# A delta-rule attention with a feed-forward block: from step 7 on most scores are computed a step later, and the queries' transposes in pairs behind later small runs

## Chip, cores, metric

One core of a Trainium2 chip runs the kernel. The metric is the device time of one execution in microseconds; runs of a kernel are given by their median. The engines are named as the profile names them: PE is TensorE (PEld its weight loads), DVE is VectorE, ACT is ScalarE, POOL is GpSimd, and SP is the queue that issues most DMAs.

## What is computed

```python
batch, n_heads, seq, head_dim = (4, 8, 768, 48)
k_n = k / (norm(k, axis=-1) + 1e-06)
state = zeros((B, H, D, D))
for t in range(S):
    y[:, :, t] = einsum('bhd,bhde->bhe', q[:, :, t], state)
    v_old = einsum('bhde,bhd->bhe', state, k_n[:, :, t])
    state = state + beta[t] * einsum('bhd,bhe->bhde', k_n[:, :, t], v[:, :, t] - v_old)
x = y.transpose(0, 2, 1, 3).reshape(B * S, H * D)      # 3072 x 384
h = x @ w_in                                           # 384 x 2048
out = (h * clip(h + 3, 0, 6) / 6) @ w_out              # 2048 x 384
```

All data are float32.

## The kernel before

**Steps.** The sequence of 768 tokens is cut into 24 chunks of 32 tokens, and one step `t` of the recurrence treats one chunk of all 4 batches and 8 heads: 4 x 32 tokens stand on the 128 partitions. Within a chunk the recurrence becomes a triangular system. What depends on the state is in `chain(t)`: the products with the state (`ks`, L795), the right hand side `R` (L890, L898), the product with the inverse (`pz`, L816, copied by ACT at L916), the update of the state (`su`, L927, subtracted by DVE at L945), the outputs (`py`, L816, added at L852), and their transposes (`yt`, L862, copied at L866). `ks`, `pz`, `py`, `su` and the scores are small matmuls, 64 rows of each in the profile; the document calls such a stretch a small run.

**Preparation.** What does not depend on the state is done six steps ahead (`LA = 6`) by `prep(t)`: POOL normalizes the keys (L499); TensorE transposes the keys and then the queries of the chunk (`pt`, L513), four transposes each, and ACT copies each result to `KQ` (L521); TensorE forms the scores of keys with keys and with queries (`sc`, L536); DVE multiplies these by a mask with beta into `L` and `LB` (L547); POOL makes that mask (`mb`, L475) and the keys times beta (`bkb`, L487). `L` goes into an inverse that is computed for a group of four chunks (`inverse`), begun in the second step of the group before; `LB` is used in the output `py`. Groups are chunk 0, then 1-4, 5-8, 9-12, 13-16, 17-20, 21-23.

**Feed-forward.** Two steps make a block of 256 tokens, `mlp_units()`. From block 3 on the first product is `up_by_eleven` (L1055): `begin(j)` takes a PSUM buffer `ph`, runs four products of 128 columns, which the profile shows as eight instructions, and hands the buffer to ACT (L1069); `end(j)` adds five more, ten instructions; DVE and ACT then read it (L1082, L1086, L1089). From block 2 on the second product is `down_by_seven` (L1215): each `product` takes one buffer `po` and comes in two halves of eight instructions, with sums on DVE (L1201) and copies on ACT (L1222).

**Order.** Everything is emitted in a fixed order, and each engine works in that order. Up to step 4 it is written out as `ORDER`. From step 5 a step has 15 units, `u` = 0 to 14. In each unit the piece of `plan` for it comes first, then some loads, some DVE work of the inverse (`fill`), and then one unit of the feed-forward. From step 7 on, in odd steps the units 0 to 11 are halves of `down_by_seven`; in even steps (from 8 on) they are `begin` and `end` in turn, `begin(2)` in unit 0, `begin(4)` in unit 4, `begin(6)` in unit 8. The plan of before, with `ch` the next piece of `chain(t)` and `now` the next piece of `prep(t + 6)`: unit 0 `ks`, then the keys' transposes and the mask; unit 2 the queries' transposes, then the load of four pieces of queries on SP; unit 4 `pz` and, directly behind it, the scores; unit 5 the multiplications and `bkb`; unit 8 `su` and `py`; unit 9 the output sum and the state; unit 10 `yt`; unit 13 the next chunk's keys are normalized. In the steps 8 and 12 (`APART`) the scores stand alone in unit 6 and the multiplications in unit 7.

**Buffers.** PSUM is used through two rings. `pm` has four buffers of one bank, for `pt`, `pz`, `py`, `yt`, `ph`, `po`; `pc` has two buffers of two banks, for `ks`, `su` and `sc`. `ring(tag, n, key)` chooses the buffer whose last user was marked read earliest in the order of emission (`read`), and the new user's first matmul then waits until the last user's readers are done. `read` notes the first mark of a key only:

```python
i = min(range(n), key=lambda i: reads.get(held[i], len(reads)))
needs(("read", held[i]))
held[i] = key
...
past.add(("read", key))
reads.setdefault(key, len(reads))
```

In `up_by_eleven` the piece that marks `ph` of `j` as read (`first`) is emitted right after `begin(j + 2)`; `py` is marked read in unit 9, `pz` with its copy in unit 4.

Of the kernel before, what the change touches and what calls it, by code (L numbers as in the profile page):

```python
# [9 lines left out]
FP32 = mybir.dt.float32  # L10
# [4 lines left out]
ACTF = mybir.ActivationFunctionType  # L15
# [29 lines left out]
def kernel(  # L45
# [55 lines left out]
    def group(t):  # L101
        return (0, t) if t < G0 else ((t - G0) // GS + 1, (t - G0) % GS)

    def size(g):
        return G0 if g == 0 else min(GS, N - first(g))

    def first(g):
        return 0 if g == 0 else G0 + (g - 1) * GS
# [35 lines left out]
    def ring(tag, n, key):  # L144

        held = rings.setdefault(tag, [])
        i = len(held)
        if i < n:
            held.append(key)
        else:  # L150
# [3 lines that stand above are left out]
        slot[tag] = f"{tag}{i}"  # L154

    def read(*keys):
        for key in keys:
            past.add(("read", key))
            reads.setdefault(key, len(reads))
# [323 lines left out]
    def scaled(t):  # L483
# [7 lines left out]
        past.add(("bkb", t))  # L491
        yield

    def prep(t, whole=True):

        g, i = group(t)
        kb, qb = kbufs[t % NKB], qbufs[t % NQB]
        needs(*([("bkb", t - NKB)] if t >= NKB else []), *(pad(t) if t < NKB and t else []))
        nc.gpsimd.tensor_tensor(  # L499
            out=kb[:, :, 0:D], in0=kfs[g][:, i],  # L500
            in1=invs.pop(t).unsqueeze(2).to_broadcast([P, H, D]), op=ALU.mult,
        )
        past.add(("kb", t))
        yield

        for j, src in enumerate((kb, qb)):
            if j == 1:
                needs(("q", t))
                past.add(("qT", t))
            ring("pm", NPM, ("pt", t, j))  # L510
            pt = psM.tile([128, NP, P], FP32, name="pt", tag=slot["pm"])
            for p in range(NP):
                nc.tensor.transpose(  # L513
                    pt[:, p, :], src[:, 2 * p : 2 * p + 2].rearrange("p e w -> p (e w)"), ident[:]
                )
            yield 1
            if j == 0:
                ring("KQ", NKQ, ("KQ", t))
                KQ = work.tile([128, NP * B // 2, 4, C], FP32, name="KQ", bufs=NKQ)
            read(("pt", t, j))  # L520
            nc.scalar.activation(  # L521
                out=KQ[:, :, 0:4:3, :] if j == 0 else KQ[:, :, 1:3, :],
                in_=pt[:].rearrange("q p (x y c) -> q (p x) y c", y=2, c=C), func=ACTF.Copy,
            )
            if whole and j == 0:
                drain(mask(t))
            yield
        ring("pc", NPC, ("sc", t))
        sc = psC.tile([P, 2, 512], FP32, name="sc", tag=slot["pc"])
        scv = sc[:, :, 0 : NP * 2 * C].rearrange("p e (a j w) -> p e a j w", a=NP, j=2)  # L530
        for p in range(NP):
            for b in range(B):
                for e in range(2):
                    r = slice(DP * e, DP * e + DP)
                    kq = KQ[r, p * B // 2 + b // 2]
                    nc.tensor.matmul(  # L536
                        scv[rows(b), e, p],
                        lhsT=kq[:, 3 if b % 2 else 0, :],
                        rhs=kq[:, 3:1:-1, :] if b % 2 else kq[:, 0:2, :],
                        start=True, stop=True,  # L540
                    )
        yield
        needs(*([("BZ", t - NLB)] if t >= NLB else []))
        LB = work.tile([P, H, C], FP32, name="LB", bufs=NLB)
        mb = mbs.pop(t)
        for j, out in enumerate((lowers(t), LB)):
            nc.vector.tensor_tensor(  # L547
                out=out.rearrange("p (e a) w -> p e a w", e=2), in0=scv[:, :, :, j, :],
                in1=mb[:, :, :, j, :], op=ALU.mult,
            )  # L550
        past.add(("L", t))
        KQs[t], LBs[t] = KQ, LB
        read(("sc", t), *([("KQ", 0)] if t == 0 else []))
        if whole:
            drain(scaled(t))
        yield
# [204 lines left out]
        yield  # L761


    xTs, outs, zs = {}, {}, {}

    def banks(name, t, i):
        ring("pc", NPC, (name, t, i))
        return psC.tile([128, 2, 512], FP32, name=name, tag=slot["pc"])

    def he(h):  # L770
        return (h % 2) * NP + h // 2
# [558 lines left out]
    def take(gen, n=1):  # L1330
        for _ in range(n):
            while next(gen, None) == 1:
                pass

    def drain(gen):
        for _ in gen:
            pass
# [103 lines left out]
    with tc.manual_schedule():  # L1441
        for word in ORDER.split():
            word, _, n = word.partition("*")
            for _ in range(int(n or 1)):
                do(word)
        for name in relus:
            settle(0, name)
        while evicts:
            evicts.pop(0)()

        units = gens["u"]
        fill = inverse_of(2)
        loads = iter(())
        left = due = 0
        USED = {"up": 0.42, "eleven": 1.0, "down": 0.7}
        APART = (8, 12)
        CHAIN = {0: 0.45, 1: 0.75, 2: 0.75, 3: 0.4, 4: 0.4, 6: 0.5, 9: 0.8, 10: 0.6, 14: 0.2}
        for t in range(LS, N):
            g, i = group(t)
            ch = chain_of(t)  # L1460
            behind = t == LS
            now, more, third, later = (prep_of(t + LA - n) for n in (2, 1, 0, -1))
            if not behind:
                now = third
            take(gens["v"], 4)
            if i == 0:
                left += 1
            if i == 2:
                loads = keys_of(g + 3)
            plan = {  # L1470
                0: lambda: take(ch),
                1: lambda: (take(ch), take(now)),
                2: lambda: (take(ch), take(now), take(gens["q"], 4)),
                3: lambda: take(ch),
                4: lambda: (take(ch), take(now, t not in APART)),
                5: lambda: take(now, t not in APART),
                6: lambda: take(now),
                7: lambda: take(now, t in APART),
                8: lambda: take(ch),
                9: lambda: take(ch),  # L1480
                10: lambda: take(ch),
                11: lambda: token_sums(t // CB),
                13: lambda: take(later),
            }
            if not behind:
                plan.update({
                    0: lambda: (take(ch), take(now)),
                    1: lambda: take(ch),
                })
            if behind:  # L1490
                plan[13] = None
                for u, gen in zip((3, 5, 5, 6, 7, 9, 10, 11, 12, 13), (more,) * 5 + (third,) * 5):
                    plan[u] = lambda old=plan.get(u), gen=gen: (old and old(), take(gen))
            ready = (1, 6)
            for u in range(NU):
                if plan.get(u):
                    plan[u]()
                take(loads, 2)
                if (i, u) == (0, 2):
                    drain(fill)  # L1500
                    left = 0
                    fill = norms_of(g + 2)
                if (i, u) == ready:
                    drain(fill)
                    fill = inverse_of(g + 1)
                    take(fill)
                    left, due = 2 * (C - 2) + 2, 0.0
                take(rest)
                take(gens["a"])
                take(units)  # L1510
                settle(1)
                while evicts:
                    evicts.pop(0)()
                if i == 1 == ready[0] and 5 < u < 7:
                    continue
                if i == 0 or not left:
                    take(fill, 2 if i or u < 2 else u > 4)
                    continue
                room = max(1.65 - USED[mode["of"]] - CHAIN.get(u, 0), 0.15) / mode["mean"]
                due += room * left / max((GS - i) * NU - u, 1)  # L1520
                due = min(due, 2.6)
                take(fill, int(due))
                left, due = max(left - int(due), 0), due - int(due)
            if behind:
                take(later)
            drain(ch)
        for _ in units:
            settle(2)
# [30 lines left out]
```

## Time and profile before

| | |
|---|---|
| median of 3 runs | 662.84 us (662.6 to 662.97) |
| the profiled execution's own time | 661.27 us |
| its span, first to last instruction | 659.6 us |
| mean granted TensorE clock | 0.984 |
| step 8 (ks to ks) | 233.33 to 258.28 us |
| step 9 | 258.28 to 283.31 us |
| step 10 | 283.31 to 308.07 us |
| last step without preparation, 20 | 529.42 to 552.56 us |

The span is what the profiler saw between the first and the last instruction. In rows by time the columns are the start, the length, the engine, the line, the operation, the output and inputs with their shapes, the count of merged instructions, and in brackets the idle time before it with what ended it. In the windows the columns are the stretch, its length, each engine's busy time with the count of instructions, the granted TensorE clock, and the DMA share. Matmuls overlap, and their ends are modelled, so the start of the next one tells more than the length of the last.

### The profile page before, as it was taken

The numbers are of one execution on the slowest core, as the hardware profiler recorded it, in microseconds if no ns is written. First come the engines' busy times: TensorE is split into PE (matmuls) and PEld (weight loads), VectorE is DVE, ScalarE is ACT, GpSimd is POOL, SyncE is SP. The second block draws the span as 40 slices with busy tenths as digits, with TensorE's granted clock in tenths as the row PEclk, the third lists the DMA queues.
The fourth block names the chain that finished last, engine by engine and source line by source line (L and its number), as shares of the span: only waits on it lengthen the run. The fifth ranks groups of instructions, "written<-read, shape, count | busy, mean of one in ns | idle before, by whom it ended". The sixth has DMA issues, their size and how long they took to land.

```text
span 659.6 us, 26613 instructions
## 1 busy us (share of the span) xinstructions
PE 631.0 (96%) x11640; PEld 567.6 (86%) x11640; DVE 501.5 (76%) x1164; ACT 263.8 (40%) x547; POOL 226.2 (34%) x352
## 2 busy tenths in 40 slices
PE   2768999999999999999999999999999999999997
PEld 2558987776689989999999999999999999999997
DVE  5989877798658988758988858989658998456354
ACT  4786578322232154154154244244243144153240
POOL 6531023003652354553254354164051242231330
PEclk9868999999999999999999999999999999999999
DMA  7889346302050030041030030030020020000101
GB/s 175 206 200 234 79 99 162 53 24 41 17 89 14 2 75 3 3 90 22 3 74 3 2 74 3 2 63 2 3 49 3 5 47 3 23 18 2 26 1 24
DMA packets 88692, 33.28 MB, mean 50 GB/s; under 512 B 80224, under 2 KB 83424, under 8 KB 88576
## 3 DMA queue, kind: packets, MB, share of 16 engines
q1 hardware_dynamic: 88224, 31.29, 21.8%
q8 instruction: 91, 1.49, 1.0%
q10 hardware_dynamic: 352, 0.30, 0.2%
q14 instruction: 25, 0.20, 0.1%
HBM read 26.84 MB, written 4.72 MB: 48 GB/s over the span
## 4 chain that ended last, share of the span: by engine, by line
PE 91%; DVE 3%; DMA 2%; SPq 1%; issue 1%; ACT 1%; DVEq 0%
PE po L1215 28%; PE ph L1055 27%; PE ph L983 9%; PE po L1151 6%; PE ks L795 4%; PE pt L513 3%; PE su L927 3%; PE pz L816 3%; PE py L816 3%; PE sc L536 2%; PE yt L862 1%; DMA w_out<-in_moe_w_in_dram 1%; SPq L168 1%; PE pi L673 1%; DMA spare<-in_moe_w_in_dram 1%
## 5 line engine op out<-in xcount | busy, mean ns | idle before, releaser
L1055 PE MATMUL ph<-xT,w_in 128*128 128x128 f32 (+1 forms) x720 | 156.3, 320 | 0.0
L1019 POOL TENSOR_TENSOR g<-g 128x256 f32<-128x256 f32 (+1 forms) x144 | 88.0, 612 | 104.0 <-ACT g L1069 98.4
L1055 PEld LDWEIGHTS ph<-xT,w_in 128*128 128x128 f32 x720 | 116.9, 191 | 6.4
L1215 PE MATMUL po<-w_out,g 128*128 128x192 f32 x640 | 110.6, 326 | 0.0
L1215 PEld LDWEIGHTS po<-w_out,g 128*128 128x128 f32 x640 | 104.6, 190 | 0.5
L1215 PE MATMUL po<-spare,g 128*128 128x192 f32 x480 | 85.1, 331 | 0.0
L1069 ACT ACTIVATE g<-ph 128x512 f32<-128x512 f32 x72 | 43.0, 597 | 92.6 <-PE ph L1055 92.6
L1215 PEld LDWEIGHTS po<-spare,g 128*128 128x128 f32 x480 | 77.4, 190 | 1.5
L983 PE MATMUL ph<-xT,w_in 128*128 128x128 f32 (+1 forms) x384 | 72.1, 338 | 0.9 <-ACT xT L866 0.6
L1225 POOL TENSOR_TENSOR o<-o,u 128x192 f32<-128x192 f32 x18 | 13.3, 741 | 163.2 <-ACT o L1222 75.6
L983 PEld LDWEIGHTS ph<-xT,w_in 128*128 128x128 f32 x384 | 59.7, 194 | 8.4 <-ACT xT L866 0.8
L1082 DVE TENSOR_TENSOR g<-ph,g 128x256 f32<-128x256 f32 x72 | 30.2, 420 | 45.7 <-PE ph L1055 41.2
L748 DVE TENSOR_TENSOR pr<-A 128x30 f32<-128x30 f32 (+9 forms) x150 | 58.4, 389 | 3.3
L1201 DVE TENSOR_TENSOR g<-g 128x512 f32<-128x512 f32 x80 | 56.2, 724 | 3.8 <-PE po L1215 3.7
L753 DVE TENSOR_TENSOR A<-A,pr 128x30 f32<-128x30 f32 (+9 forms) x150 | 56.3, 375 | 3.3
L1102 DVE SCALAR_TENSOR_TENSOR g<-o,g 128x512 f32<-128x512 f32 x72 | 52.5, 729 | 7.4 <-ACT o L1099 7.4
L1055 PE MATMUL ph<-beta_tok,sums_in 128*128 128x128 f32 x288 | 55.7, 275 | 0.0
L1099 ACT ACTIVATE o<-g 128x512 f32<-128x512 f32 x72 | 45.4, 630 | 11.8 <-DVE g L1102 8.5
L1222 ACT ACTIVATE o<-po 128x192 f32<-128x192 f32 x40 | 13.2, 330 | 90.8 <-PE po L1215 90.8
L345 ACT ACTIVATE spare<-spare 128x768 uint16<-128x768 uint16 (+1 forms) x56 | 47.3, 850 | 3.1 <-DVE X L547 1.8
L499 POOL TENSOR_TENSOR kb<-kf,inv 128x384 f32<-128x384 f32 x24 | 21.7, 906 | 73.2 <-issue 42.6
L1151 PE MATMUL po<-w_out,g 128*128 128x384 f32 x128 | 45.4, 490 | 0.0
(137 smaller groups left out, 1010.2 us busy)
## 6 DMA issues: line engine op xcount, KB each, us to landing
kf<-in_k_dram SPq DMA_DIRECT2D x96, 48.0 KB, 2.8
qb<-in_q_dram SPq DMA_DIRECT2D x96, 48.0 KB, 2.6
vf<-in_v_dram SPq DMA_DIRECT2D x96, 48.0 KB, 2.4
out_dram<-o SPq DMA_DIRECT2D x90, 48.0 KB, 1.6
spare<-in_moe_w_in_dram SPq DMA_DIRECT2D x4, 768.0 KB, 5.4
w_out<-in_moe_w_in_dram SPq DMA_DIRECT2D x4, 768.0 KB, 6.1
w_out<-in_moe_w_out_dram SPq DMA_DIRECT2D x4, 768.0 KB, 7.4
spare<-in_moe_w_out_dram SPq DMA_DIRECT2D x4, 768.0 KB, 5.5
```

Source lines behind the costliest of these rows:

```text
L345: nc.scalar.activation(out=z, in_=z if n else d.bitcast(I16)[:, :, :, 3], func=func, bias=value, scale=scale,)
L748: nc.vector.tensor_tensor(out=pv, in0=A[:, j + 1 :, j].unsqueeze(2).to_broadcast([n, w, j]), in1=A[:, j, 0:j].unsqueeze(1).to_broadcast([n ...
L753: nc.vector.tensor_tensor(out=A[:, j + 1 :, 0:j], in0=A[:, j + 1 :, 0:j], in1=pv, op=ALU.subtract)
L983: nc.tensor.matmul(ph[:, cols], lhsT=w_in[:, s, f * 128 : (f + 1) * 128], rhs=xT[:, s, cols], start=(s == 0), stop=(s == NKT - 1),)
L1019: nc.gpsimd.tensor_tensor(out=out, in0=a, in1=b, op=op)
L1055: nc.tensor.matmul(ph[:, n], lhsT=w, rhs=x, start=start, stop=stop, skip_group_check=True)
L1069: nc.scalar.activation(out=gt, in_=ph[:], func=ACTF.Copy)
L1099: nc.scalar.activation(out=r, in_=g, func=ACTF.Relu, bias=0.5, scale=1.0 / 6.0)
L1102: nc.vector.scalar_tensor_tensor(out=g, in0=r, scalar=1.0, in1=g, op0=ALU.min, op1=ALU.mult)
L1151: nc.tensor.matmul(pos[c][:], lhsT=gs[blk, f // 2][:, f % 2, c * P : (c + 1) * P], rhs=w_out[:, f, :], start=(f == 0), stop=(f == NFC - 1),)
L1201: nc.vector.tensor_tensor(out=A(f, *out, 4), in0=A(f, *a, 4), in1=A(f, *b, 4), op=op)
L1215: nc.tensor.matmul(ps[n][:], lhsT=A(f - f % 2, *a)[:, f % 2], rhs=b[:, f], start=(f == 0), stop=(f == HF - 1),)
```

## The change

`late(t)` picks the chunks after 11 that are not the last of their group: 13, 14, 15, 17, 18, 19, 21, 22. For these:

- The queries' transposes come in two pairs, each with a `pm` buffer of its own and an ACT copy of 256 columns in place of one of 512. The first pair stands in unit 4 behind `pz`, the second in unit 8 behind `py`; the mask is made behind the second.
- The scores come in unit 0 of the next step, behind `ks` and ahead of that step's keys' transposes. The multiplications and `bkb` come in unit 5 of the next step (in unit 7 of the steps 8 and 12).
- The scores no longer use `pc`. The two buffers of `pc` are now allocated once (`halves_of_banks`); `ks` and `su` use columns 0 to 255 of each bank, late scores columns 256 to 511 by a ring of their own, `ps`. Scores that are not late still use `pc`, in columns 0 to 255.
- The load of queries moves from unit 2 to unit 9 in these steps.
- In the steps 10, 14 and 17, which prepare the last chunk of a group, the late scores of the chunk before it stand in unit 0, their multiplications and the next mask in unit 3, and the own scores behind `pz` as before.

```diff
+    def late(t):
+        g, i = group(t)
+        return LS + LA < t < first(g) + size(g) - 1
+
...
-                past.add(("qT", t))
+                if not late(t):
+                    past.add(("qT", t))
+            if j == 1 and late(t):
+                n = NP // 2
+                for p0 in range(0, NP, n):
+                    ring("pm", NPM, ("pt", t, p0))
+                    pt = psM.tile([128, n, P], FP32, name="pt", tag=slot["pm"])
+                    for p in range(n):
+                        p2 = 2 * (p0 + p)
+                        nc.tensor.transpose(
+                            pt[:, p, :], src[:, p2 : p2 + 2].rearrange("p e w -> p (e w)"), ident[:]
+                        )
+                    yield 1
+                    read(("pt", t, p0))
+                    x = B // 2
+                    nc.scalar.activation(
+                        out=KQ[:, x * p0 : x * p0 + x * n, 1:3, :],
+                        in_=pt[:].rearrange("q p (x y c) -> q (p x) y c", y=2, c=C), func=ACTF.Copy,
+                    )
+                    if p0:
+                        past.add(("qT", t))
+                        drain(mask(t))
+                    yield
+                break
             ring("pm", NPM, ("pt", t, j))
...
-            if whole and j == 0:
+            if whole and j == 0 and not late(t) and not late(t - 1):
                 drain(mask(t))
             yield
-        ring("pc", NPC, ("sc", t))
-        sc = psC.tile([P, 2, 512], FP32, name="sc", tag=slot["pc"])
+        tag, c = ("ps", 256) if late(t) else ("pc", 0)
+        ring(tag, NPC, ("sc", t))
+        sc = halves_of_banks[int(slot[tag][2:])][:, :, c : c + 256]
...
+    halves_of_banks = [psC.tile([128, 2, 512], FP32, name=f"pc{i}") for i in range(NPC)]
...
-        return psC.tile([128, 2, 512], FP32, name=name, tag=slot["pc"])
+        return halves_of_banks[int(slot["pc"][2:])][:, :, 0:256]
...
             if not behind:
+                last = prep_of(t + LA - 1) if late(t + LA - 1) else iter(())
                 plan.update({
-                    0: lambda: (take(ch), take(now)),
+                    0: lambda: (take(ch), take(last), take(now)),
                     1: lambda: take(ch),
                 })
+                if late(t + LA):
+                    plan.update({
+                        2: lambda: take(ch),
+                        4: lambda: (take(ch), take(now)),
+                        5: lambda: take(last, t not in APART),
+                        6: None,
+                        7: lambda: take(last, t in APART),
+                        8: lambda: (take(ch), take(now)),
+                        9: lambda: (take(ch), take(gens["q"], 4)),
+                    })
+                elif late(t + LA - 1):
+                    plan[3] = lambda: (take(ch), take(last), drain(mask(t + LA)))
```

## The prediction, made before the changed kernel was run

> **What bounds the kernel now.** I read the page first, then the chain of waits, then TensorE's order of time in the steps that the change touches.
>
> ```profile
> span 659.6 us, 26613 instructions
> PE 631.0 (96%) x11640; PEld 567.6 (86%) x11640; DVE 501.5 (76%) x1164; ACT 263.8 (40%) x547; POOL 226.2 (34%) x352
> PE 91%; DVE 3%; DMA 2%; SPq 1%; issue 1%; ACT 1%; DVEq 0%
> ```
>
> TensorE is busy 96% and is 91% of the chain. In the windows of single steps it never rests at all, at full clock, while ScalarE (ACT) works half the time:
>
> ```profile
> core 0: us, PE busy (x) PEld busy (x) DVE busy (x) ACT busy (x) POOL busy (x), PEclk, DMA share, GB/s
> 40.00:50.00 10.00, 6.10 (x210) 5.14 (x209) 8.35 (x15) 8.15 (x13) 2.35 (x6) 0.78 0.79 214
> 60.00:80.00 20.00, 19.14 (x669) 17.65 (x669) 17.85 (x49) 13.28 (x33) 2.14 (x4) 1.00 0.37 102
> 233.30:258.30 25.00, 25.00 (x470) 22.76 (x469) 21.64 (x52) 12.20 (x26) 14.80 (x22) 1.00 0.24 46
> 383.10:407.85 24.75, 24.75 (x466) 22.81 (x465) 18.05 (x41) 12.20 (x26) 13.97 (x23) 1.00 0.22 40
> ```
>
> So in these steps only two things count: what TensorE's order costs, and any new wait of TensorE. Step 8 (233.3 to 258.3) shows the price of the order. A row's second number is a modelled end; I use differences of starts.
>
> ```profile
> 234.41 0.66 PE L513 MATMUL pt<-ident,kb 128*128 128x128 f32 x4
> 234.90 0.39 PE L1055 MATMUL ph<-xT,w_in 128*128 128x128 f32 x2
> ...
> 237.33 0.60 PE L513 MATMUL pt<-ident,qb 128*128 128x128 f32 x4
> 237.76 0.39 PE L1055 MATMUL ph<-xT,w_in 128*128 128x128 f32 x2
> ...
> 240.28 0.88 PE L816 MATMUL pz<-R,X 32*32 32x48 f32 x64
> 241.10 0.49 PE L1055 MATMUL ph<-xT,w_in 128*128 128x128 f32 x2
> ...
> 243.72 0.86 PE L536 MATMUL sc<-KQ 64*32 64x64 f32 x64
> 244.51 0.49 PE L1055 MATMUL ph<-xT,w_in 128*128 128x128 f32 x2
> ...
> 247.13 0.89 PE L927 MATMUL su<-R,bkb 32*64 32x48 f32 x64
> ```
>
> Eighteen large matmuls (one `begin`, one `end`) stand in each gap. From transposes to transposes they take 237.33 - 234.90 = 2.43; from transposes to a small run 240.28 - 237.76 = 2.52; between two small runs 243.72 - 241.10 = 2.62. **Entering a small run costs 0.09, leaving it for large matmuls 0.10.** Four transposes on their own take 237.76 - 237.33 = 0.43, behind a small run 234.90 - 234.41 = 0.49: leaving a small run for transposes costs 0.06.
>
> **What the order saves.** `late` holds for eight targets: 13, 14, 15, 17, 18, 19, 21, 22, prepared in steps 7, 8, 9, 11, 12, 13, 15, 16. Their scores move from behind `pz` to behind the next step's `ks`: both places are inside a small run, so their 0.79 (243.72 to 244.51) is only moved. The exceptions are steps 8 and 12, where the scores stood alone: one entry and one exit less, 0.19 each, **-0.38**. Half of the queries' transposes leave `pz`, the other half `py`; an exit at 0.10 becomes one at 0.06, which is -0.08 a step. All of it would be 0.38 + 8 x 0.08 = 1.0 us saved. One wait of before also goes: in step 16 eighteen large matmuls lead from `py` to `yt` (448.13 to 450.81, 2.68, where step 8 has 248.76 to 251.29, 2.53): **-0.15**, since the new pair of transposes in between gives VectorE that time.
>
> ```profile
> 448.13 0.49 PE L1055 MATMUL ph<-xT,w_in 128*128 128x128 f32 x2
> ...
> 450.81 0.52 PE L862 MATMUL yt<-ident,y 128*128 128x128 f32 x3
> ...
> 248.76 0.49 PE L1055 MATMUL ph<-xT,w_in 128*128 128x128 f32 x2
> ...
> 251.29 0.49 PE L862 MATMUL yt<-ident,y 128*128 128x128 f32 x3
> ```
>
> **What the pairs cost: a buffer.** Each pair takes a `pm` buffer, of which there are four, right before the next `begin` (steps 8, 12, 16) or `product` (odd steps). `ring` gives the next user the buffer whose key was marked read first. The first pair's key is ("pt", t, 0), the key that the keys' transposes already used and that was marked read at unit 0; `read` keeps the first mark. So the pair's buffer counts as the oldest at once, and the product at unit 4 gets just this one, in odd steps (where older ones are free) as in even ones. At unit 8 of the even steps two of the four hold open `ph` tiles (`begin(6)` comes before `first(4)` is emitted), `py` is not marked until unit 9, and `begin(6)` gets the second pair's buffer. In both places TensorE must sit until ScalarE has copied the pair. Before, one small product stood before each `begin` and an older buffer was left. The price, from step 10 and the early stage:
>
> ```profile
> 287.32 0.60 PE L513 MATMUL pt<-ident,qb 128*128 128x128 f32 x4
> 287.75 0.39 PE L1055 MATMUL ph<-xT,w_in 128*128 128x128 f32 x2
> 287.95 0.60 ACT L521 ACTIVATE KQ<-pt 128x512 f32<-128x512 f32 x1 [0.55 <-PE pt L513]
> ...
> 288.85 0.60 ACT L1069 ACTIVATE g<-ph 128x512 f32<-128x512 f32 x1 [0.30 <-PE ph L1055]
> 289.34 0.27 ACT L1089 ACTIVATE g<-ph 128x128 f32<-128x128 f32 x1
> ...
> 291.09 0.86 PE L536 MATMUL sc<-KQ 64*32 64x64 f32 x64
> 291.23 0.49 ACT L916 ACTIVATE R<-pz 128x384 f32<-128x384 f32 x1 [0.48 <-PE pz L816]
> ```
>
> ```profile
> 49.77 0.49 ACT L866 ACTIVATE xT<-yt 128x384 f32<-128x384 f32 x1 [0.64 <-PE yt L862]
> 50.32 1.36 PE L983 MATMUL ph<-xT,w_in 128*128 128x128 f32 x8 [0.58 <-ACT xT L866]
> ```
>
> ```profile
> L990 ACT ACTIVATE g<-ph 128x256 f32<-128x256 f32 x32 | 12.2, 382 | 32.4 <-PE ph L983 32.4
> ```
>
> A copy starts 0.20 after the transposes' successor would (287.75 to 287.95); TensorE starts 50.32 - 50.26 = 0.06 after a copy's end; a copy of 256 columns takes 0.38 (the nearest form). **Unit 4**, counted from where `pz` is left: the pair is done at 0.06 + 0.43/2 = 0.27. ScalarE works in the order of the program, and the copy of `pz` stands first: it starts at 0.14 (291.09 to 291.23) and ends at 0.63. The pair's copy can start 0.10 ahead of that end (289.34 against 288.85 + 0.60), so it ends at 0.91 and TensorE goes on at **0.97**, 0.70 idle. The restart costs the 0.10 of an exit. **Unit 8**: 0.27 + 0.20 + 0.38 + 0.06 = **0.91** after `py`, 0.64 idle.
>
> Against before, an odd late step loses 0.43 (the old transposes), gains 0.97 at unit 4, and 0.27 - 0.10 at unit 8: +0.71. An even one: -0.43 + 0.97 + 0.91 = +1.45. Five odd and three even: 3.55 + 4.35 = 7.9; less 0.38 and 0.15 the sum is **+7.4 us**. From below: without these waits 0; from above: no overlap of the two copies and the 0.60 of a 512 column copy would add 0.3 to each of 11 waits, +3.3. I take the 256 column row, whose shape is that of the pair.
>
> **What sharing a buffer costs.** Scores, `ks` and `su` are now pieces of one tile. Whether a write of columns 0 to 255 waits for a read of columns 256 to 511 is not shown before, since there each user had the tile alone. What is shown is that `su` is held by the multiplication of the scores that stood in its buffer:
>
> ```profile
> 343.51 0.86 PE L536 MATMUL sc<-KQ 64*32 64x64 f32 x64
> ...
> 345.99 0.42 DVE L547 TENSOR_TENSOR L<-sc,mb 128x256 f32<-128x256 f32 x1
> 346.33 0.41 DVE L547 TENSOR_TENSOR LB<-sc,mb 128x256 f32<-128x256 f32 x1
> 346.92 0.76 PEld L927 LDWEIGHTS su<-R,bkb 32*64 32x64 f32 x64 [0.33 <-DVE LB L547]
> ```
>
> In step 12 `LB` ends at 346.74, 3.32 after the matmuls before the scores (343.51 less 0.09). With the scores gone `su` would come 2.52 after these; if held, at 3.32 + 0.06: 0.86 lost, in steps 8 and 12 (in the others the multiplication is at unit 5). In step 17 scores 23 fall on the buffer whose other half VectorE then reads for 22, behind the output sums:
>
> ```profile
> 465.07 0.74 DVE L808 SCALAR_TENSOR_TENSOR y<-ks,parity,y 128x192 f32<-128x192 f32 x2
> 465.13 0.88 PE L816 MATMUL pz<-R,X 32*32 32x48 f32 x64
> 465.95 0.86 PE L536 MATMUL sc<-KQ 64*32 64x64 f32 x64
> ```
>
> It would end near 465.81 + 0.74, 0.6 after 465.95. So 0 to 2 x 0.86 + 0.6 = 2.3; by the order through the buffer in the rows above I take **+2.3**.
>
> The Trainium skill, "PSUM — Partial Sum Buffer", section "PSUM bank collisions raise a hardware error", says that two engines on one bank and quadrant collide even at disjoint columns, so that software has to order them by bank; by that the upper end holds, by columns alone 0. No row before decides it.
>
> **At nothing.** ScalarE gets two copies of 0.38 for one of 0.60, in a step in which it works 12.2 of 24.8 us. The mask (1.19 on POOL) goes from unit 0 to unit 8, ahead of `begin(6)`'s sums; POOL idles 2.96 there, and uncovered it would cost that step up to 1.2. The query loads go from unit 2 to unit 9 on SP's queue, four steps before they are used; the value and key loads ahead of them wait for nothing new. `bkb` and the two multiplications come one step later, still before the inverse, whose last targets are not late.
>
> ```profile
> 284.83 1.19 POOL L475 TENSOR_TENSOR mb<-beta_tok,mask 128x256 f32<-128x256 f32 x2
> ...
> 300.42 0.73 POOL L1019 TENSOR_TENSOR g<-g 128x256 f32<-128x256 f32 x1 [2.96 <-ACT g L1069]
> ```
>
> **Forecast.** 661.27 + 7.4 + 2.3 = 671.0 for the profiled execution; the median of the runs is 1.57 above that execution, so 662.84 + 9.7 = **672.5 us**, 1.5% slower.
>
> **Rivals.** (1) Halves are ordered by columns: 662.84 + 7.4 = 670.2. (2) The product at unit 4 waits for the copy of `pz` alone (0.63 + 0.06 = 0.69 in place of 0.97, 8 x 0.28 = 2.2 less): 668.0 to 670.3; against it speaks the repeated key. (3) **The other side:** the pairs' buffers are not the ones asked for next, and only the order counts. It decides where an older buffer is free at units 4 and 8, as before the change at each `begin`, where the step's windows show no idle TensorE. Then 8 x 0.08 + 0.38 + 0.15 = 1.2 is saved: 661.6. (4) The mask or the later multiplications collide with `begin`'s sums in each late step: 8 x 0.6, half of the 1.2 above, 677. (5) The granted clock falls, as at 40 to 50 us, where TensorE worked 6.1 of 10 us at 0.78: eight steps of 25 us at 0.78 would add 56 us. An even late step would have 0.70 + 0.64 + 0.86 idle in about 27, 92% busy, nearer to the row at 60 to 80 us (19.14 of 20, clock 1.00).
>
> The Trainium skill, "TensorE: Matmul & The Clock Gate", section "A second HAM failure mode: psum-queue depth-cycling", warns that cycling PSUM buffers with frequent short idles makes the clock swing; that is rival (5), and the 1.00 at 60 to 80 us speaks against it here.
>
> **How the numbers follow.** Forecast 0.54, rivals (1) 0.17, (2) 0.10, (3) 0.13, (4) 0.04, (5) 0.02. The range 667.0 to 675.0 holds the forecast, (1) and (2), 0.81, and up to 2.5 for copies that overlap less. A measurement of this kernel tells 0.2%, 1.3 us, from no change; (3) at -1.2 lies just on this bound and is split, as copies may take less than I count: faster 0.08, same 0.05, slower 0.87.
>
> **What would show it.** Right: TensorE's starts at unit 4 of all eight late steps 0.7 late behind `pt` with ScalarE's `KQ` copy as releaser; the same at unit 8 of steps 8, 12, 16 only; `su` held by `LB` in 8 and 12; no stall in steps 10, 14 and from 18. Odd late steps near 25.0 + 0.7, even ones 1.2 to 2.3 longer. Wrong: products that start directly behind the pairs, then (3); a release by the copy of `pz`, then (2); a PEclk below 1.00 in these steps, then (5).

## The result, and the profile after

| | before | after |
|---|---|---|
| median, six runs each on one chip | 662.51 us | 673.47 us |
| the profiled execution's own time | 661.27 us | 670.73 us |
| its span | 659.6 us | 669.0 us |

The changed kernel is 1.6% slower: 1.0164 of the time before, 95% interval 1.0136 to 1.0192. The page of the profile after says where to look. Its first lines, TensorE's clock over the 40 slices, and two of the costliest groups (behind the last bar: idle time of the engine just before the group, and what ended it):

```profile
span 669.0 us, 26608 instructions
PE 635.6 (95%) x11640; PEld 570.0 (85%) x11640; DVE 501.5 (75%) x1164; ACT 264.5 (40%) x555; POOL 231.2 (35%) x352
...
PEclk9559999999999999999999999999999999999999
...
L1084 PE MATMUL ph<-xT,w_in 128*128 128x128 f32 (+1 forms) x720 | 155.2, 320 | 2.8 <-ACT KQ L528 2.8
...
L1244 PE MATMUL po<-spare,g 128*128 128x192 f32 x480 | 84.6, 330 | 2.6 <-ACT KQ L528 2.6
```

ScalarE's copy of the queries (`KQ`, L528) has become the releaser of the feed-forward's products, 2.8 + 2.6 us in all. The clock row stands at 9, which is 90% or more, in every slice of the changed steps. The windows from the start of step 7 to the start of step 18 (from `ks` to `ks`), first after and then before; the clock in them is 1.00:

```profile
207.10:491.74 284.64, 276.90 (x5044) 257.09 (x5044) 223.24 (x503) 97.59 (x217) 119.42 (x166) 1.00 0.13 25
```

```profile
208.28:482.87 274.59, 274.59 (x5045) 256.86 (x5044) 220.97 (x503) 97.28 (x209) 112.15 (x163) 1.00 0.14 27
```

The stretch takes 284.64 in place of 274.59 us, 10.05 more, with the same matmuls (5044 and 5045 records). TensorE, which never rested there, is idle for 284.64 - 276.90 = 7.74. The other 2.3 stands in rows that count as busy: ends of matmuls are modelled, and a wait costs more than its idle time shows (the hold of `su` below, in which TensorE stands until VectorE has read, costs 1.38 and shows 1.10). Ahead of step 7 and behind step 17 the kernels differ by -1.18 and +0.6 in these two executions; step 7 began anywhere from 207.1 to 209.9 in the runs below, so I leave that out.

The instructions in order of time show the three kinds of wait. Step 9, unit 4; then step 8, units 4 and 8; then step 17:

```profile
267.33 0.88 PE L845 MATMUL pz<-R,X 32*32 32x48 f32 x64
268.14 0.44 PE L522 MATMUL pt<-ident,qb 128*128 128x128 f32 x2
268.28 0.49 ACT L945 ACTIVATE R<-pz 128x384 f32<-128x384 f32 x1 [0.51 <-PE pz L845]
268.66 0.38 ACT L528 ACTIVATE KQ<-pt 128x256 f32<-128x256 f32 x1
...
269.09 1.08 PE L1244 MATMUL po<-spare,g 128*128 128x192 f32 x5 [0.52 <-ACT KQ L528]
```

```profile
239.40 0.88 PE L845 MATMUL pz<-R,X 32*32 32x48 f32 x64
240.30 0.41 PE L522 MATMUL pt<-ident,qb 128*128 128x128 f32 x2
...
241.18 0.49 PE L1084 MATMUL ph<-xT,w_in 128*128 128x128 f32 x2 [0.47 <-ACT KQ L528]
...
245.48 1.26 POOL L1048 TENSOR_TENSOR g<-g 128x256 f32<-128x256 f32 x2 [1.17 <-ACT g L1098]
245.62 0.79 DVE L781 TENSOR_TENSOR A<-A,pr 128x184 f32<-128x184 f32 x1
246.23 0.32 PE L956 MATMUL pc<-R,bkb 32*64 32x48 f32 x4
...
246.70 0.92 POOL L487 TENSOR_TENSOR bkb<-kb,beta_tok 128x384 f32<-128x384 f32 x1
...
247.18 0.41 DVE L575 TENSOR_TENSOR LB<-pc,mb 128x256 f32<-128x256 f32 x1
247.65 0.85 PE L956 MATMUL pc<-R,bkb 32*64 32x48 f32 x60 [1.10 <-DVE LB L575]
248.43 0.88 PE L845 MATMUL py<-R,LB 32*32 32x48 f32 x64
249.24 0.44 PE L522 MATMUL pt<-ident,qb 128*128 128x128 f32 x2
...
250.16 0.49 PE L1084 MATMUL ph<-xT,w_in 128*128 128x128 f32 x2 [0.47 <-ACT KQ L528]
```

```profile
473.19 0.74 DVE L837 SCALAR_TENSOR_TENSOR y<-pc,parity,y 128x192 f32<-128x192 f32 x2
...
474.01 0.88 PE L845 MATMUL pz<-R,X 32*32 32x48 f32 x64
...
474.18 0.42 DVE L575 TENSOR_TENSOR LB<-pc,mb 128x256 f32<-128x256 f32 x1
...
474.68 0.99 POOL L475 TENSOR_TENSOR mb<-beta_tok,mask 128x256 f32<-128x256 f32 x1 [10.24 <-DVE LB L575]
...
474.82 0.86 PE L564 MATMUL pc<-KQ 64*32 64x64 f32 x64
```

`pz` takes 0.81 of TensorE's order (267.33 to 268.14). In step 9 the product begins 269.09 - 268.14 = 0.95 behind it. In step 8 `begin` comes 241.18 - 240.21 = 0.97 behind `pz` (239.40 + 0.81), though the pair itself stands at 240.30, and 250.16 - 249.24 = 0.92 behind `py` and the second pair's start. Between these, four matmuls of `su` (now named `pc<-R,bkb`) get through at 246.23 and the other 60 stand until `LB` has read the other columns of their buffer: `py` comes 248.43 - 246.23 = 2.20 behind `su`'s start, where an unheld `su` takes 0.82, as in step 8 before the change (247.13 to 247.95). In step 17 the scores stand 0.81 behind `pz`'s start, so directly behind it, and nothing holds them.

By steps (differences of the starts of `ks`; the scores' 0.79 leaves the steps 7, 11, 15 and arrives in 10, 14, 17):

| step | before | after | e1_key | e2_mult5 | e3_both | e4_halves | e8_yt11_mask12 | e12_swap |
|---|---|---|---|---|---|---|---|---|
| 8 | 24.95 | 27.58 | 27.29 | 26.20 | 25.91 | 25.74 | 24.75 | 24.75 |
| 9 | 25.04 | 25.73 | 24.98 | 25.73 | 25.06 | 24.97 | 25.03 | 25.02 |
| 11 | 25.04 | 24.94 | 24.16 | 24.94 | 24.16 | 24.16 | 24.16 | 24.16 |
| 12 | 24.95 | 27.59 | 27.30 | 26.20 | 25.91 | 26.15 | 24.75 | 24.75 |
| 13 | 25.04 | 25.73 | 24.95 | 25.73 | 24.95 | 24.95 | 25.47 | 24.95 |
| 14 | 24.75 | 25.55 | 25.56 | 25.55 | 25.56 | 25.55 | 25.56 | 25.56 |
| 16 | 24.94 | 26.20 | 25.90 | 26.20 | 25.91 | 26.16 | 24.75 | 25.00 |
| 17 | 25.04 | 25.83 | 25.83 | 25.83 | 25.83 | 25.83 | 25.83 | 25.83 |
| 7 to 17 | 274.58 | 284.64 | 279.83 | 281.86 | 277.15 | 277.38 | 274.17 | 273.89 |

### The profile page after: what moved, and what is told of

Its sections match the earlier page's. It is cut to its first block, busy times and chain, and to the rows that moved or that the text cites. A ratio compares the mean times of both kernels' runs of the same rounds, so it can differ in the third digit from the quotient of the medians.

```text
span 669.0 us, 26608 instructions
## 1 busy us (share of the span) xinstructions
PE 635.6 (95%) x11640; PEld 570.0 (85%) x11640; DVE 501.5 (75%) x1164; ACT 264.5 (40%) x555; POOL 231.2 (35%) x352
## 4 chain that ended last, share of the span: by engine, by line
PE 90%; DVE 4%; ACT 3%; issue 1%; SPq 1%; DMA 0%; POOL 0%; ACTq 0%; DVEq 0%
PE po L1244 28%; PE ph L1084 26%; PE ph L1012 9%; PE po L1180 6%; PE pc L824 4%; PE pt L540 3%; PE pc L956 3%; PE pz L845 3%; PE py L845 3%; PE pc L564 3%; PE yt L891 1%; ACT spare L345 1%; PE pi L701 1%; ACT R L945 1%; SPq L168 1%
```

## The experiments

Each kernel was run beside the kernel before on its chip, and ratios are to that. The first three undo one cost each.

**e1_key.** The first pair gets a key of its own, so its buffer no longer counts as the one read longest ago.

```diff
-                    ring("pm", NPM, ("pt", t, p0))
+                    ring("pm", NPM, ("pt", t, 1 + p0))
...
-                    read(("pt", t, p0))
+                    read(("pt", t, 1 + p0))
```

> The changed kernel with a key of its own for the first pair of the queries' transposes, nothing else. If the repeated key makes that pair's buffer count as the oldest: in the odd late steps (7, 9, 11, 13, 15) the product of unit 4 starts directly behind the pair, 0.27 after pz in place of 0.95, and without the 0.10 of a restart, so step 9 falls from 25.73 to 24.95; in the even ones (8, 12, 16) begin(4) gets the buffer of pz and waits for its copy, 0.69 after pz in place of 0.97, so 0.28 less. Together 5 x 0.78 + 3 x 0.28 = 4.7 us less than the changed kernel: ratio to before about 1.009. If four buffers are simply too few for a pair and a product in one unit, whatever the key: no change, step 9 stays at 25.73 and the ratio at 1.016.

Measured: 667.1 us, ratio 1.0091 (1.0071 to 1.0111), steps 7 to 17 4.81 shorter than after the change. Step 9, unit 4, in order of time:

```profile
268.82 0.41 PE L522 MATMUL pt<-ident,qb 128*128 128x128 f32 x2
268.90 0.49 ACT L945 ACTIVATE R<-pz 128x384 f32<-128x384 f32 x1 [0.51 <-PE pz L845]
268.96 0.19 PEld L1244 LDWEIGHTS po<-spare,g 128*128 128x128 f32 x1
```

The product's weights load 0.14 behind the pair, while ScalarE still copies `pz`. The repeated key was worth 0.75 to 0.83 in each odd step. In even steps only 0.29 to 0.30 comes back: `begin` now gets the buffer of `pz` and waits for its copy. In step 8 it starts at 241.81, 0.05 behind that copy's end. The group of `begin` and `end` shows both waits that the even steps still have:

```profile
L1084 PE MATMUL ph<-xT,w_in 128*128 128x128 f32 (+1 forms) x720 | 155.3, 320 | 2.0 <-ACT KQ L528 1.4 <-ACT R L945 0.5
```

**e2_mult5.** The multiplications of steps 8 and 12 go from unit 7 to unit 5, where the other steps have them.

```diff
-                        5: lambda: take(last, t not in APART),
+                        5: lambda: take(last),
...
-                        7: lambda: take(last, t in APART),
+                        7: None,
```

> The changed kernel with the multiplications of the late scores at unit 5 in steps 8 and 12 too (they stood at unit 7 there). If su is held there because its buffer's other columns are still being read: the 1.39 us inside su goes in both steps, su takes 0.82 as in the others, steps 8 and 12 fall from 27.58 to about 26.2, the whole 2.8 us less than the changed kernel, ratio about 1.012. If columns are ordered apart and the hold has another cause (the output LB, or bkb on POOL): su stays at 2.20 and nothing changes.

Measured: 669.06 us, ratio 1.0118 (1.0098 to 1.0138). Step 8:

```profile
244.58 0.41 DVE L575 TENSOR_TENSOR LB<-pc,mb 128x256 f32<-128x256 f32 x1
...
247.61 0.89 PE L956 MATMUL pc<-R,bkb 32*64 32x48 f32 x64
```

`LB` is done 2.6 ahead of `su`, `su` runs in one piece, and steps 8 and 12 are as long as step 16. The hold was 27.58 - 26.20 = 1.38 a step. The edit moves `bkb` along with the multiplications; that `LB` and not `bkb` was the releaser is what the profile names (`247.65 ... <-DVE LB`).

**e3_both.** Both edits together.

> Both edits at once: a key of its own for the first pair, and the multiplications at unit 5. If the two costs are separate they add: 4.7 + 2.8 = 7.5 us less than the changed kernel, ratio about 1.005; what stays above the kernel before are the two waits of the even steps (begin(4) on the copy of pz, begin(6) on that of the second pair). If one hides behind the other, the sum is smaller than its parts.

Measured: 664.97 us, ratio 1.0062 (1.0041 to 1.0082). The savings add up, but for 0.10: 7.49 in steps 7 to 17, where 4.81 and 2.78 were seen alone. What is left stands in the even steps, 25.91 each: the two waits of `begin`.

**e4_halves.** The pairs take no `pm` buffer any more. They use the free columns 256 to 511 of one bank of the tile with the even `ks`, and late scores those of the odd one; multiplications in unit 5.

```diff
-                    ring("pm", NPM, ("pt", t, p0))
-                    pt = psM.tile([128, n, P], FP32, name="pt", tag=slot["pm"])
+                    pt = halves_of_banks[1 - odd_at[0]][:, 0, 256:512].rearrange(
+                        "q (p w) -> q p w", p=n
+                    )
...
+        at = odd_at[0] if late(t) else int(slot[tag][2:])
+        sc = halves_of_banks[at][:, :, c : c + 256]
...
+            odd_at[0] = int(slot["pc"][2:])
```

> Both pairs leave the ring of four buffers: they use the free columns of the bank pair that holds the first products with the state, late scores the free columns of the other; multiplications at unit 5. Theory: no product waits for a pair's copy, only the order counts, 8 x 0.08 + 0.38 + 0.15 = 1.2 us less than the kernel before: ratio 0.998, late steps 9 and 11 near 24.95, 8, 12 and 16 near 24.7. Rival: the shared bank makes new waits (the pair for the output sums that read the products with the state, the state's subtraction for the pair's copy), then 0.3 to 0.8 us in each late step, ratio 1.002 to 1.008.

Measured: 664.6 us, ratio 1.0047 (1.0027 to 1.0068). No product waits for a pair, yet steps 12 and 16 are longer than in e3_both. What was expected as the other possibility, a wait of TensorE at the shared bank, isn't there either. There is a third thing, here in step 12:

```profile
333.62 1.15 PE L827 MATMUL pc<-state,KQ 64*64 64x48 f32 x64
...
338.71 0.42 DVE L1114 TENSOR_TENSOR g<-ph,g 128x256 f32<-128x256 f32 x1 [1.49 <-PE ph L1087]
...
350.73 0.89 DVE L777 TENSOR_TENSOR pr<-A 128x150 f32<-128x150 f32 x1
352.07 0.54 DVE L884 TENSOR_TENSOR y<-y,py 128x384 f32<-128x384 f32 x1
...
352.76 0.52 PE L894 MATMUL yt<-ident,y 128*128 128x128 f32 x3 [1.22 <-DVE y L884]
```

TensorE's transposes `yt` wait 1.22 for VectorE's output sum, 352.07 - 333.62 = 18.45 after the step's start. In step 8 before it came 250.16 - 233.33 = 16.83 after:

```profile
250.16 0.55 DVE L852 TENSOR_TENSOR y<-y,py 128x384 f32<-128x384 f32 x1
```

VectorE is late, and until now TensorE's own waits had covered that: in step 12 of the changed kernel the sum began 18.42 after the step's start, and `yt` not until 20.61. The expectations below put the waits of steps 8, 12 and 16 at 0.96, 1.38 and 1.38, which is about what they add to the steps; the idle times are 0.80, 1.22 and 1.22. Two causes were possible: the scores' place ahead of the step's first `begin`, or the mask on GpSimd that now runs beside VectorE's work on the inverse.

**e5_scores.** Only the scores are late; the queries' transposes stay whole in unit 2. The mask is made in unit 8, the multiplications in unit 5.

```diff
-                        2: lambda: take(ch),
-                        4: lambda: (take(ch), take(now)),
+                        2: lambda: (take(ch), take(now), take(gens["q"], 4)),
+                        4: lambda: take(ch),
...
```

> Only the scores move: late scores behind the next step's products with the state, in the free columns; the queries' transposes stay whole in unit 2, in one buffer of the ring; the mask is made in unit 8, the multiplications at unit 5. By the order of the small runs alone 0.19 is saved in steps 8 and 12 and nothing in the others: steps 9 and 13 at 25.04, 8 and 12 at 24.76, ratio 0.999. If instead the lateness of VectorE that held yt in the version with pairs in the free columns comes from the mask in unit 8, yt waits here too, and longer, as no pair stands between py and yt: 1.0 to 1.6 us in steps 8, 12 and 16, ratio about 1.005.

Measured: 664.41 us, ratio 1.0047 (1.0028 to 1.0066), steps 8, 12 and 16 at 26.14 to 26.17. Steps 12 and 16 are as long as in e4_halves, step 8 is 0.40 longer, and `yt` waits for the output sum in all three (1.19 to 1.22). So the wait comes without the pairs too.

**e6_yt11.** e4_halves with `yt` one unit later in even late steps, behind the next products.

```diff
+                    if t % CB == 0:
+                        plan.update({10: None, 11: lambda: take(ch)})
```

> The version with the pairs in the free columns, with yt in unit 11 in place of 10 in the even late steps. If yt only came too early for VectorE's output sum there: the waits of 0.96, 1.38 and 1.38 in steps 8, 12 and 16 go, these steps fall to about 24.7, steps 7 to 17 together to 273.6 (before: 274.6), ratio 0.998 to 1.000. If VectorE is behind by more than a unit, a part of the wait stays, or a later user of its results waits in turn (the products with the state, the token sums).

Measured: 661.95 us, ratio 1.001 (0.9992 to 1.0029). Steps 8, 12, 16 take 24.79, 25.20, 25.20; the wait is gone in step 8, and 0.24 is left in steps 12 and 16.

**e7_mask12.** e4_halves with the mask made in unit 12.

```diff
-                        drain(mask(t))
...
+                drain(mask(t))
+                yield
...
+                        12: lambda: take(now),
```

> The version with the pairs in the free columns, with the mask of the late chunks made in unit 12 in place of 8 and yt in unit 10 again. If the mask on POOL lengthens VectorE's instructions that run beside it and so delays the output sum: the waits of yt in steps 8, 12, 16 (0.96, 1.38, 1.38) shrink by more than half, ratio about 1.001. If VectorE just has too many instructions ahead of the output sum: the waits stay within 0.2 of what they were.

Measured: 663.81 us, ratio 1.003 (1.0015 to 1.0045). In step 12 the wait falls to 0.69:

```profile
332.37 1.15 PE L828 MATMUL pc<-state,KQ 64*64 64x48 f32 x64
...
350.29 0.54 DVE L885 TENSOR_TENSOR y<-y,py 128x384 f32<-128x384 f32 x1
...
350.98 0.52 PE L895 MATMUL yt<-ident,y 128*128 128x128 f32 x3 [0.69 <-DVE y L885]
```

The output sum comes 350.29 - 332.37 = 17.92 after the step's start, 0.53 earlier than in e4_halves, and the wait is shorter by the same: the mask's place is less than half of it. Step 16 gains as much; in step 8, where the wait was 0.80, it is only 0.13.

**e8_yt11_mask12.** Both of these together.

> Pairs in the free columns, multiplications at unit 5, yt in unit 11 of the even late steps and the mask in unit 12. If the lateness of VectorE is partly the mask's (0.5 of 1.38 in steps 12 and 16) and the later yt covers the rest: the waits of 0.3 that yt still had in steps 12 and 16 go, steps 8, 12, 16 near 24.75, steps 7 to 17 together 273.7 (before: 274.6), ratio 0.998 to 0.999. If not, 274.7 as with the mask in unit 8, ratio 1.001.

Measured: 661.04 us, ratio 0.9999 (0.9986 to 1.0012). Steps 8, 12, 16 now take 24.75, with no wait of `yt`. But step 13 takes 25.47, since `pz` waits there:

```profile
363.52 0.61 DVE L931 SCALAR_TENSOR_TENSOR R<-pc,parity,R 128x384 f32<-128x384 f32 x1
363.99 0.33 ACT L1255 ACTIVATE o<-po 128x192 f32<-128x192 f32 x1 [0.37 <-PE po L1248]
...
364.41 0.88 PE L849 MATMUL pz<-R,X 32*32 32x48 f32 x64 [0.45 <-ACT o L1255]
```

`pz` reads `R`, which is done at 364.13. The row names ScalarE's copy, which ends at 364.32. In steps 9 and 17 of this run `pz` starts ahead of the like copy, and 0.15 and 0.19 behind `R`; that speaks for `R`, and so for VectorE being late here too, but the two were not separated.

**e9_pair9.** From e3_both: in even late steps the second pair comes in unit 9, behind `begin(6)`, so that `begin(6)` doesn't get its buffer.

```diff
+                    if t % CB == 0:
+                        plan.update({
+                            8: lambda: take(ch),
+                            9: lambda: (take(ch), take(now), take(gens["q"], 4)),
+                        })
```

> The version with a key of its own and the multiplications at unit 5, with the second pair in unit 9 of the even late steps, behind begin(6) in place of ahead of it. If the wait of 0.64 at unit 8 is begin(6) on that pair's copy alone: begin(6) starts directly behind py, the pair costs its 0.22 and the exit 0.10 falls to py, 0.59 less in steps 8, 12, 16: 25.3 in place of 25.91, 1.8 us together. VectorE's output sum ended 0.3 to 0.6 ahead of yt there, so part of it can come back as a wait of yt, up to 0.3 in step 16. If the wait has another cause (py, the state), these steps stay at 25.9.

Measured: 666.46 us, ratio 1.0083 (1.0064 to 1.0101): steps of 26.29, worse than the 25.91 of e3_both. A miss. The pair itself now waits for a buffer that ScalarE reads:

```profile
251.56 0.44 PE L522 MATMUL pt<-ident,qb 128*128 128x128 f32 x2 [0.85 <-ACT g L1118]
```

Four buffers, with two `ph` tiles open, left one user waiting in either place.

**e10_scores4.** e4_halves, but in steps 8, 12 and 16 the late scores stand behind `pz`.

```diff
+                    if t % CB == 0:
+                        plan.update({
+                            0: lambda: (take(ch), take(now)),
+                            4: lambda: (take(ch), take(last), take(now)),
+                        })
```

> e4_halves, but in steps 8, 12 and 16 the late scores stand directly behind pz in unit 4 (one whole step late, in the place that they have in step 16 before the change) and no longer in unit 0. If VectorE's output sum was late because the scores stood ahead of the step's first begin, so that the ph tiles that VectorE reads in program order came 0.8 later, then VectorE reaches the output sum near 17.2 after the step's start (as in step 16 before) in place of 18.04, the wait of yt falls from 0.96, 1.38, 1.38 to under 0.5, steps 12 and 16 take 24.8 to 25.2 in place of 26.15, steps 7 to 17 about 274.3 in place of 277.38, ratio 0.999 to 1.002. Rival: VectorE was late because its inverse runs beside the mask and bkb on GpSimd; then the wait stays near 1 and the steps near 25.7 to 26.2, ratio 1.004.

Measured: 664.65 us, ratio 1.0046 (1.0027 to 1.0064). Steps 25.76, 25.82, 26.48: neither was right, as the edit made a wait of its own. The idle time ahead of `yt` is down to 0.05 and 0.10 in steps 8 and 12, and 0.77 in step 16, but the scores wait now. Step 8:

```profile
240.18 0.74 DVE L840 SCALAR_TENSOR_TENSOR y<-pc,parity,y 128x192 f32<-128x192 f32 x2 [0.41 <-ACT y L864]
...
240.98 0.86 PE L565 MATMUL pc<-KQ 64*32 64x64 f32 x64 [0.79 <-DVE y L840]
...
247.48 1.39 POOL L475 TENSOR_TENSOR mb<-beta_tok,mask 128x256 f32<-128x256 f32 x2
247.77 0.63 DVE L777 TENSOR_TENSOR pr<-A 128x168 f32<-128x168 f32 x1
```

The scores write columns 256 to 511 and stand 0.79 until VectorE has read columns 0 to 255 of the same buffer (the odd `ks`).

**e11_scores4_mask12.** The same with the mask in unit 12.

> The same with the mask in unit 12 as in e7_mask12. By the order of the scores no wait of yt is left: steps 8, 12, 16 near 24.8, steps 7 to 17 near 273.8, ratio 0.998 to 1.000. By the rival nothing beyond e7_mask12: steps near 25.6, ratio 1.003.

Measured: 662.84 us, ratio 1.0028 (1.001 to 1.0045), steps 25.53, 25.53, 25.77. The instruction beside which the mask ran in step 8 is short again:

```profile
247.00 0.33 DVE L778 TENSOR_TENSOR pr<-A 128x168 f32<-128x168 f32 x1
```

The scores still wait 0.79 for the odd read, so the place of the scores could not be judged from these two.

**e12_swap.** The last edit is to take that wait away: in these three steps the scores and the pairs change tiles, so the scores write beside the even `ks`, which is read earlier.

```diff
             odd_at[0] = int(slot["pc"][2:])
+            if t > 0 and t % CB == 0 and late(t + LA):
+                odd_at[0] = 1 - odd_at[0]
```

> e11_scores4_mask12, but in steps 8, 12 and 16 the late scores take the free columns of the tile with the even ks and the pairs those of the odd one. In e10_scores4 the scores waited 0.8 for VectorE's read (y, odd) of the other columns of their bank; the even tile is read to its end by ScalarE's y, 7.4 after the step's start, and the scores come at 7.3, the pair at 8.2 behind the odd read's end at 8.1. If the wait goes by the bank, the scores start directly behind pz, and the step is 0.7 to 0.9 shorter unless VectorE's output sum is late again: it came at 17.8 in e11_scores4_mask12 and would have to come by about 17.2; had the hold of the scores itself made it late (begin's sums 0.6 later), it does. Then steps 8, 12, 16 take 24.7 to 25.0 in place of 25.53 to 25.77, ratio 0.998 to 1.000. If VectorE is late by its own, yt waits 0.5 to 0.8, the steps stay at 25.2 to 25.6, ratio 1.001 to 1.003. If the hold isn't the bank's, the scores still wait for VectorE's y (odd).

Measured: 660.96 us against 661.21, ratio 0.9996 (0.9986 to 1.0005). Step 12:

```profile
331.71 1.15 PE L830 MATMUL pc<-state,KQ 64*64 64x48 f32 x64
...
336.01 0.43 DVE L1117 TENSOR_TENSOR g<-ph,g 128x256 f32<-128x256 f32 x1
...
348.75 0.55 DVE L887 TENSOR_TENSOR y<-y,py 128x384 f32<-128x384 f32 x1
349.48 0.49 PE L897 MATMUL yt<-ident,y 128*128 128x128 f32 x3
```

The first expected case came about: the scores wait no more, so the wait went by the buffer and not by the scores' place alone. VectorE reads the first `ph` 336.01 - 331.71 = 4.30 after the step's start, where e4_halves had 338.71 - 333.62 = 5.09: the scores' 0.79. It does the output sum 17.04 after it in place of 18.45, and `yt` waits no more in steps 8 and 12; in step 16 it comes 0.22 later than there. VectorE works in program order, so scores ahead of the first `begin` can make everything behind that `begin`'s sums late. Of the 1.41 at the output sum the mask's place is 0.53 (e7_mask12), and 0.88 goes with the place of the scores and the tiles (e7_mask12 to e12_swap, 17.92 to 17.04). How much of this 0.88 is the place's and how much the tiles' was not separated. Scores behind `pz` without that wait, but with the mask in unit 8, were not tried.

## Why the prediction was right

The predicted time was 672.5 us, the median is 673.47, inside the range. By steps 7 to 17, predicted +9.7 and seen +10.06. The waits at units 4 and 8 came as predicted. Two terms of the shared buffer missed, by +1.04 and -0.6, and that they partly cancel is luck:

- **Unit 4: right in cause and size.** Predicted was a release by ScalarE's `KQ` copy 0.97 behind `pz`; seen are 0.95 in step 9 and 0.97 in step 8. Odd late steps were to gain 0.71; they gained 0.69 in steps 9 and 13 and, with the scores' 0.79 put back, 0.74 in step 7 and 0.69 in steps 11 and 15. e1_key shows that the repeated key is the cause, so rival (2), a wait for the copy of `pz` alone, is out for the changed kernel; that wait is what even steps fall back to once the key is mended.
- **Unit 8: right.** Predicted 0.91, seen 0.92. Step 16, which has both waits and no hold of `su`, was to gain 1.45 - 0.15 = 1.30 and gained 1.26.
- **The shared buffer: right in cause, too small.** The term of 0.86 a step measured 1.38 (e2_mult5), 1.04 more over two steps. `su` did wait for a read of other columns, so the halves are not ordered by columns. The step that was off took the end of `LB` from the time before. It came later, as VectorE's inverse ran beside GpSimd ahead of it: in step 8 the row of 184 columns took 0.79 and the next, of 168, 0.48; before the change they took 0.35 and 0.33 there. That is 0.59 of lateness for 0.52 of miss. The first row before:

```profile
245.54 0.35 DVE L753 TENSOR_TENSOR A<-A,pr 128x184 f32<-128x184 f32 x1
```

- **Step 17: wrong.** The 0.6 was 0. Without the 0.79 of the scores of 22, which moved into it, the step is as long as before. I took VectorE's place against `pz` from the time before, where the output sums began 0.06 ahead of it. After the change they began 474.01 - 473.19 = 0.82 ahead, since the scores of 22 now stand ahead of `pz` on TensorE, and `LB` was done at 474.60, before the scores came at 474.82.
- **"At nothing": true only under cover.** But for the hold of `su`, the mask and the later multiplications cost nothing in the changed kernel, because TensorE stood still longer than VectorE was late: from the step's start, the output sum began at 18.42 in step 12 and `yt` at 20.61, in step 16 at 18.31 and 19.22. The prediction named 1.2 as the price of the mask uncovered; e7_mask12 shows 0.53 in step 12. The larger part, 0.88, which goes with the scores' place and the tiles, was in no term and no rival.
- **The order's saving: seen in the steps, and small.** With the waits for pairs and the holds out of the way, e12_swap takes 273.89 for steps 7 to 17, 0.69 less than before; the other side had 1.2. Steps 8 and 12 save 0.20 each, as 0.19 + 0.08 said within 0.07. Most of what is missing is in step 16, 0.06 longer than before where 0.15 + 0.08 was to go. By the ratio's interval the whole can't be told from no change.
- **The clock** stayed at 1.00 in the window. The Trainium skill, "TensorE: Matmul & The Clock Gate", section "A second HAM failure mode: psum-queue depth-cycling", tells of a kernel in which frequent short idles, as it cycled through PSUM banks, made the clock swing. Idle times of 0.5 to 1.1 us, 13 in 285 us, did not do so here.

## What to carry to other kernels

Where a ring hands out the buffer that was marked read first, look at which key a new user marks: a key that was used before makes its buffer the first to be handed out, and a stall arises where free buffers stand idle. When work is moved ahead in TensorE's order, follow the engines that read behind it in program order to their next hand-over to TensorE; the delay may show only after the nearer waits are gone. The two column halves of a buffer were one resource for waits here (`su` behind `LB` 1.38, scores behind the odd read 0.79; whether by the bank or by the whole buffer of two banks, no run separates), so put together what is read at the same time.

## What was not expected of the hardware

VectorE's instructions on the inverse, both of whose inputs lie in SBUF, took 0.33 to 0.35 us for 168 to 184 columns alone (e11_scores4_mask12, before) and 0.63 to 0.79 with a two-input GpSimd instruction beside them (e10_scores4, after). It isn't always VectorE that loses: a row of 198 columns took 0.36 at 318.58 after the change, beside GpSimd's sum `o<-o,u` from 318.34, which itself took 1.05 there where its median is 0.70 (spans on GpSimd are rough). An instruction with an input in PSUM did not stretch: `LB` took 0.41 at 247.18, with `bkb` on GpSimd beside it, and 0.42 at 474.18, where GpSimd rested.
